# Three of four first layers by quarter products from the second group on, their weights' differences taken earlier, and some output adds done by DMA

## The chip, the core and the metric

The kernel runs on one core of a Trainium2 chip. The core has five engines with a queue of instructions each, worked off in order: TensorE (PE: matmuls into PSUM, with PEld for its weight loads), VectorE (DVE), ScalarE (ACT), GpSimd (POOL) and SyncE (SP), which here only issues DMAs. Engines meet through semaphores. The metric is the device time of one execution in microseconds (us); lower is better.

## The reference

Two stages. First, attention for 8 batches and 8 heads: 512 local tokens with a window of 32 to each side, plus 32 global tokens that see all and are seen by all. Second, a mixture of 8 experts on its output, with routing weights P from a Sinkhorn iteration:

```python
k_all = np.concatenate([k_g, k_l], axis=2); v_all = np.concatenate([v_g, v_l], axis=2)
out_g = np.matmul(sm(scale * q_g @ k_all.T), v_all)
s_ll = np.where(np.abs(pos[:, None] - pos[None, :]) <= 32, scale * q_l @ k_l.T, -1e9)
a_l = sm(np.concatenate([scale * q_l @ k_g.T, s_ll], axis=-1))
x = concat(out_g, a_l @ v_all)            # 4352 tokens, 512 wide
P = np.exp(x @ w_gate - max)
for _ in range(8):
    P /= P.sum(1, keepdims=True) + 1e-09
    P /= P.sum(0, keepdims=True) + 1e-09
    P *= N / E
for e in range(8):                        # w1[e]: 512 x 1024, w2[e]: 1024 x 512
    out += P[:, e:e + 1] * (np.maximum(x @ w1[e], 0.0) @ w2[e])
```

## The kernel before

**First part, about 0 to 374 us.** Attention runs in slots `s` of some 10.3 us, one pair of heads of one batch each (`HP` = 4 slots a batch, `NU` = 32). The matmuls of a slot are filled up with first layers of experts 0 to 3, one eighth at a time (`f1`, `p_l1`, L461 to L475); such a hidden tile `hT` (8 KB a partition, pool `hpool`, four buffers) is stored to DRAM (`hd`) when it is full. ScalarE and VectorE take the outputs in turn. SP issues the loads of queries and keys (`load_qk`, L122), of values (L166 to L172) and the hidden stores (L475), all in one queue. GpSimd issues the loads that change the type, among them `load_w1d` (L484): the first-layer weights of experts 4 to 7 are copied to DRAM in fp16 (`w1d`), one expert a batch from slot 13 on, in the order 4, 5, 6, 7. The Sinkhorn iterations follow, with the rest of the first layers beside them.

**Second part, about 374 us to the end.** Tokens come in groups `m` of 512 (0 to 7) and a last one of 256. Within a group the units (group, expert) come in `ORDER = (4, 0, 5, 1, 6, 2, 7, 3)`, that is in pairs (4,0), (5,1), (6,2), (7,3). The first unit of a pair computes its hidden layer now, the second loads it from `hd`. I call the body of the loop for the first unit the first half of the pair, for the second unit the second half. Everything is scaled by the routing weight `pb` on the way: the input `xs` (`scale_x`) or the loaded `h` (`scale_h`). The order of each engine's work is the order in which the loop body at the end writes it out.

The second layer is a 2x2 Strassen form: seven products (`product`, matmuls at L928) of h or sums and differences of halves of h (`sums`, VectorE at L689) with prepared weights `w2c`. Products 1 to 5 of a whole group accumulate in five fixed PSUM banks `m1` to `m5`; products 6 and 7 share rotating banks (`pm`) over the two units of a pair, so they are run back to back at a pair's middle: last in the first half, first in the second. `add` (L933) brings a finished bank into the output tile `o`: products 6 and 7 after each pair, products 1 to 5 once, after the pair (7,3) (`closes`). An add is one VectorE instruction (L944), and a first write is ScalarE's (L942). So ten VectorE adds stand together at the second half of (7,3): two for products 6 and 7, eight for the fixed banks. GpSimd then stores `o` (L947).

The first layer has two forms. The plain one, `l1` (L812), takes 32 matmuls of 512 columns a unit. The other, class `Fast` (L822), does it by quarter products: seven products of 256 columns for each half p of the hidden width, 56 matmuls of 256 columns in all. It needs weights as seven prepared quarters (`w1c`, in DRAM) and differences of quarters of `xs` (`sums_x`, four VectorE operations). A half p is done in four steps, s0 to s3, between the second-layer products:

```python
def s1(self):
    self.mul(self.K, 2, False, True)
    self.relu(self.K, 0, 0)
    self.mul(self.H, 6, False, True)
    self.X = self.tile("r1")
    nc.vector.tensor_tensor(out=self.X, in0=self.H, in1=self.t5, op=ALU.add)

def s2(self):
    self.mul(self.H, 7, False, True)
    self.mul(self.X, 3, False, True)
```

The VectorE add (L861) reads bank H, and the next matmuls of s2 add onto the same bank, so they wait for it. L868 is the second such add. A unit is `fast` from the group on that `WX` gives: experts 6 and 7 from group 2, twelve units in all. Half p = 0 of the next first unit is run in the first half of the pair ahead of it, half p = 1 in the second half. The prepared quarters are made in group 1: `load_w1` brings raw quarters, `prep_w1` (L735) takes four sums a piece on VectorE, and GpSimd stores them to `w1c`.

Of the kernel before, what the change touches and what calls it, by code (L numbers as in the profile page):

```python
# [9 lines left out]
FP16 = mybir.dt.float16  # L10
FP32 = mybir.dt.float32
AF = mybir.ActivationFunctionType
ALU = mybir.AluOpType
# [10 lines left out]
def kernel(  # L24
# [26 lines left out]
    HP = H // 2  # L51
    DP = D // P
    FT = F // P
    NT = NTOK // P
# [5 lines left out]

    persist = ctx.enter_context(tc.tile_pool(name="persist", bufs=1))
    lg = persist.tile([P, NT, E], FP32)
    wg_sb = persist.tile([P, DP, E], FP16)
    ones_f = persist.tile([P, P], FP32)
    identity = persist.tile([P, P], FP16)
# [5 lines left out]
    NL = E // 2  # L73
# [1 line left out]
    xd = [ydram.tile([P, DP, n], FP16, name=f"xd{m}") for m, (_, n) in enumerate(groups)]  # L75
    w1d = [ydram.tile([P, DP, F], FP16, name=f"w1d{e}") for e in range(NL, E)]
    pd = ydram.tile([E, NTOK], FP32, name="pd")
    WX = {6: 2, 7: 2}
    w1c = {e: [ydram.tile([P, 7, 2, 256], FP16, name=f"w1c{e}_{p}") for p in range(2)] for e in WX}
    psx = ExitStack()  # L80
    xpool = psx.enter_context(tc.tile_pool(name="xpool", bufs=1, side="right"))
    xT = [xpool.tile([P, DP, n], FP16, name=f"xT{m}") for m, (_, n) in enumerate(groups)]

    skp = ctx.enter_context(tc.tile_pool(name="skp", bufs=2))
    pss = ExitStack()
    ps_mm = pss.enter_context(tc.tile_pool(name="ps_mm", bufs=2, space=PSUM))
    ps_sc = pss.enter_context(tc.tile_pool(name="ps_sc", bufs=2, space=PSUM))
# [4 lines left out]
    with tc.tile_pool(name="att_c", bufs=1) as att_c, \  # L92
# [308 lines left out]
        def st_G1(b, g):  # L401
            n0 = HP * b + 2 * g
            qg = qgbd[(2 * b + g) % 2]
            gc = slice(Sg * b, Sg * (b + 1))
            sg = ps_po.tile([P, 2 * 512], FP32, tag="po")
            for c0, c1, k0 in ((0, Sl - W, 2 * W), (Sl - W, Sl, W), (Sl, S, None)):
                for pr in range(2):
                    rhs = kgT[:, 2 * g + pr, gc] if k0 is None else kTe[(n0 + pr) % NK][:, k0 : k0 + c1 - c0]
                    nc.tensor.matmul(sg[:, c0:c1], qg[:, pr, :], rhs, start=(pr == 0), stop=(pr == 1))
            m2 = att_wk.tile([P, 4], FP32, tag="m2")  # L410
            nc.vector.reduce_max(out=m2[:, 0:1], in_=sg[:, 0:S], axis=AX.X)  # L411
            nc.vector.tensor_scalar(out=m2[:, 1:2], in0=m2[:, 0:1], scalar1=-scale, scalar2=None, op0=ALU.mult)
# [64 lines left out]
        def load_w1e(e):  # L477
# [2 lines left out]
            wts[e] = pool.tile([P, DP, F], FP16, name="w1e", **kw)  # L480
            nc.gpsimd.dma_start(out=wts[e], in_=moe_w1[e].rearrange("(dko dki) f -> dki dko f", dki=P))

        def load_w1d(e):
            nc.gpsimd.dma_start(out=w1d[e - NL], in_=moe_w1[e].rearrange("(dko dki) f -> dki dko f", dki=P))  # L484

        fill = [(k % NL, k // NL) for k in range(NL * (B + 1))]
        n1 = 0
# [100 lines left out]
        for s in range(HP, NU + 1):  # L588
# [99 lines left out]
    def tt(out, in0, in1, op):  # L688
        nc.vector.tensor_tensor(out=out, in0=in0, in1=in1, op=op)  # L689
# [21 lines left out]
    raw = {}  # L711
    wnext = 0

    def load_w1(used):
        nonlocal wnext
        while wnext < len(wseq) and (wnext < 2 or wseq[wnext - 2] in used):
            i, *p = wseq[wnext]
            if p[0] is None:
                w = w1s[i] = wpool.tile([P, DP, F], FP16, tag="w1e", name="w1s")
                nc.sync.dma_start(out=w, in_=w1d[units[i][1] - NL])  # L720
            else:
                w = wpool.tile([P, 7, 2, 256], FP16, tag="w1e", name="w1q")
                if p[0] == "raw":
                    for o, r, k in ((0, 0, 0), (1, 0, 1), (3, 1, 0), (2, 1, 1)):
                        f0 = 512 * r + 256 * p[1]
                        nc.sync.dma_start(out=w[:, o], in_=w1d[i - NL][:, 2 * k : 2 * k + 2, f0 : f0 + 256])
                    raw[wseq[wnext]] = w
                else:
                    nc.sync.dma_start(out=w, in_=w1c[units[i][1]][p[0]])
                    w1s[(i, p[0])] = w  # L730
# [12 lines left out]

    def load_pb(*us):
        us = [i for i in us if i < NUN]
# [187 lines left out]
    def add(i, q, pm):  # L933
        m, e = units[i]
        nt = groups[m][1] // P // 2
        if m not in os_:
            os_[m] = ypool.tile([P, NJ, D], FP32, tag="y", name="o")
        for j, (r, d, sg) in enumerate(QUARTER[q]):
            o = os_[m][:, nt * r : nt * (r + 1), HD * d : HD * (d + 1)]
            p = pm[:, 0 : HD * nt].rearrange("p (t d) -> p t d", d=HD)  # L940
            if (q >= 6 and e == ORDER[1]) or (q in (3, 4) and j == 0):
                nc.scalar.mul(o, p, 1.0 / float(E))  # L942
            else:
                nc.vector.scalar_tensor_tensor(out=o, in0=p, scalar=sg / float(E), in1=o, op0=ALU.mult, op1=ALU.add)  # L944
# [128 lines left out]
    for i, (m, e) in enumerate(units):  # L1073
        if i == NUN - 1:
            last_pair(i)
        elif i % 2 == 0:
# [44 lines left out]
            else:  # L1121
# [92 lines left out]
```

## Time and profile before

| | us |
|---|---|
| median of 3 runs | 1045.3 |
| range of the runs | 1044.04 to 1048.0 |
| the profiled execution | 1044.08 |
| its span on the engines | 1042.2 |
| PE busy | 1015.2 |
| DVE busy | 868.7 |
| ACT busy | 513.0 |
| POOL busy | 139.7 |

The busy time of an engine is what its instructions took; matmuls overlap, so PE's is modelled. The prediction shows rows of four kinds. The page's first part gives busy time and share of the span. A window row gives, for a stretch of the span, its length, the busy time of each engine with its number of instructions, the TensorE clock that was granted (1.00 is full), the busy share of the DMA engines and GB/s. A timeline row gives start, length, engine, line, operation, output and inputs with sizes, how many were merged, and in brackets how long the engine had stood idle and what ended that.

### The profile page before, as it was taken

How to read it: one execution, taken by the hardware profiler on the slowest of the kernel's cores; microseconds unless marked ns; L12 is line 12 of the kernel's file. 1: busy time of each engine (PE TensorE's matmuls, PEld its weight loads, DVE VectorE, ACT ScalarE, POOL GpSimd, SP SyncE). 2: the span in 40 equal slices, each digit the busy share in tenths (PEclk: the TensorE clock that was granted, in tenths of full speed). 3: DMA queues.
4: the chain of work that ended last, by engine and by line, in shares of the span. 5: the costliest groups of instructions: out<-in, count | busy, mean ns of one | idle time of the engine just before them, and what ended most of it. 6: DMA issues, size and time to landing. Idle time of an engine off the chain costs nothing.

```text
span 1042.2 us, 22693 instructions
## 1 busy us (share of the span) xinstructions
PE 1015.2 (97%) x9142; PEld 728.5 (70%) x9142; DVE 868.7 (83%) x1638; ACT 513.0 (49%) x1296; POOL 139.7 (13%) x227
## 2 busy tenths in 40 slices
PE   7899999999999999999999999999999999999998
PEld 4555555555555466777777877877877878878887
DVE  7687777777776786999889799889899898898895
ACT  7777878787876675223222333333333332332331
POOL 7442423414312102000000000000000000000000
PEclk9899999999999999999999999999999999999999
DMA  9887588988945999946756546454553555464470
GB/s 260 197 217 207 118 273 181 220 232 177 258 136 142 275 261 302 259 143 203 272 194 234 189 153 219 160 189 180 200 189 138 203 187 168 172 218 152 145 260 26
DMA packets 101960, 206.08 MB, mean 198 GB/s; under 512 B 33936, under 2 KB 68192, under 8 KB 90592
## 3 DMA queue, kind: packets, MB, share of 16 engines
q1 hardware_dynamic: 56064, 162.75, 45.1%
q0 software_dynamic: 43184, 32.26, 17.7%
q10 hardware_dynamic: 2608, 9.64, 2.4%
q8 instruction: 71, 1.16, 0.4%
q14 instruction: 33, 0.27, 0.1%
HBM read 168.64 MB, written 57.29 MB: 217 GB/s over the span
## 4 chain that ended last, share of the span: by engine, by line
PE 83%; ACT 8%; DVE 6%; issue 2%; DMA 1%; SPq 0%; POOL 0%; ACTq 0%; DVEq 0%
PE m L928 28%; PE ph L818 15%; PE ph L468 15%; PE pm L928 11%; PE pf L836 7%; ACT Pu L311 4%; DVE Pu L348 3%; PE ptw L359 1%; ACT hT L471 1%; ACT qbd L285 1%; PE pv L157 1%; PE pt L275 1%; DMA vraw<-in_v_l_dram 1%; PE po L380 1%; DVE m L411 1%
## 5 line engine op out<-in xcount | busy, mean ns | idle before, releaser
L468 PE MATMUL ph<-xT,w1e 128*128 128x512 f16 (+1 forms) x1152 | 255.9, 367 | 0.2
L928 PEld LDWEIGHTS <-h 128*128 128x128 f16 x2160 | 211.4, 98 | 36.6
L820 ACT ACTIVATE h<-ph 128x512 f16<-128x512 f32 (+1 forms) x192 | 107.5, 562 | 204.2 <-PE ph L818 202.2
L928 PE MATMUL m<-w2c,s 128*128 128x256 f16 x1620 | 199.9, 273 | 0.0
L928 PEld LDWEIGHTS <-s 128*128 128x128 f16 x1620 | 158.5, 98 | 30.5
L818 PE MATMUL ph<-xs,w1s 128*128 128x512 f16 (+1 forms) x768 | 174.6, 361 | 0.0
L468 PEld LDWEIGHTS <-w1e 128*128 128x128 f16 x1152 | 105.4, 98 | 96.1 <-issue 3.0
L689 DVE TENSOR_TENSOR h<-h,pb 128x2048 f16<-128x2048 f16 (+1 forms) x48 | 152.4, 3175 | 3.8 <-DMA h<-hd 3.7
L689 DVE TENSOR_TENSOR s<-h 128x1024 f16<-128x1024 f16 (+2 forms) x166 | 126.4, 803 | 24.3 <-PE m L928 16.9
L928 PE MATMUL m<-w2c,h 128*128 128x256 f16 x1080 | 137.2, 273 | 0.0
L471 ACT ACTIVATE hT<-ph 128x512 f16<-128x512 f32 (+1 forms) x192 | 104.4, 559 | 47.5 <-PE ph L468 45.2
L928 PE MATMUL pm<-w2c,h 128*128 128x256 f16 x1080 | 123.8, 273 | 0.0
L818 PEld LDWEIGHTS <-w1s 128*128 128x128 f16 x768 | 75.1, 98 | 52.6
L843 ACT ACTIVATE h<-pf 128x512 f16<-128x512 f32 x96 | 55.0, 596 | 84.1 <-PE pf L836 79.9
L311 ACT ACTIVATE Pu<-ms,mx 128x160 f16<-128x160 f32 x224 | 93.6, 420 | 5.2 <-DVE mx L308 2.7
L473 DVE TENSOR_SCALAR hT<-ph 128x512 f16<-128x512 f32 x96 | 66.1, 688 | 31.3 <-PE ph L468 30.5
L689 DVE TENSOR_TENSOR h<-h 128x1024 f16<-128x1024 f16 (+1 forms) x166 | 90.3, 586 | 0.0
L689 DVE TENSOR_TENSOR xs<-xg,pb 128x2048 f16<-128x2048 f16 (+1 forms) x36 | 78.1, 2169 | 12.8 <-DMA pb<-pd 12.8
L947 POOL DMA_DIRECT2D out_dram<-o x8 | 6.1, 758 | 533.3 <-DVE o L944 533.3
L308 DVE CUSTOM_DVE_ANT_0 ms<-sc,mask 128x160 f32<-128x160 f32 x224 | 59.9, 319 | 18.7 <-PE sc L303 18.2
L836 PEld LDWEIGHTS <-w1q 128*128 128x128 f16 x672 | 65.7, 98 | 7.7
L852 ACT COPY pf<-pf 128x512 f32<-128x512 f32 x24 | 13.7, 570 | 81.5 <-PE pf L836 81.5
(165 smaller groups left out, 1225.7 us busy)
## 6 DMA issues: line engine op xcount, KB each, us to landing
h<-hd SPq DMA_DIRECT2D x32, 1024.0 KB
hd<-hT SPq DMA_DIRECT2D x26, 1024.0 KB
w1s<-w1d SPq DMA_DIRECT2D x24, 1024.0 KB
w1q<-w1c SPq DMA_DIRECT2D x24, 896.0 KB
pb<-pd SPq DMA_DIRECT2D x64, 256.0 KB
w2c<-in_moe_w_dram POOLq DMA_DIRECT2D x16, 512.0 KB, 20.1
out_dram<-o POOLq DMA_DIRECT2D x8, 1024.0 KB, 4.6
f<-in_q_l_dram SPq DMA_DIRECT2D x15, 512.0 KB
```

The costliest lines, as they stand in the source:

```text
L308: nc.vector.tensor_tensor_reduce(out=ms[:, ii, :], in0=sc[:, SW * ii : SW * (ii + 1)], in1=mask[:, mi, :], scale=-scale, scalar=BIG, op0=A ...
L311: nc.scalar.activation(out=d["Pu"][:, i, :], in_=ms[:, ii, :], func=AF.Exp, scale=-1.0, bias=d["mx"][:, i : i + 1], accum_out=d["sm"][:, i ...
L348: nc.vector.tensor_tensor(out=d["Pu"][:, i0:i1, 0:KW], in0=d["Pu"][:, i0:i1, 0:KW], in1=d["rs"][:, i0:i1].unsqueeze(2).to_broadcast([P, i1 ...
L468: nc.tensor.matmul(ph[:, 0:n], wts[e][:, dk, P * fm : P * (fm + 1)], xT[m][:, dk, :], start=(dk == 0), stop=(dk == DP - 1))
L471: nc.scalar.activation(out=hT[:, fm, 0:n], in_=ph[:, 0:n], func=AF.Relu)
L473: nc.vector.tensor_scalar(out=hT[:, fm, 0:n], in0=ph[:, 0:n], scalar1=0.0, scalar2=None, op0=ALU.max)
L689: nc.vector.tensor_tensor(out=out, in0=in0, in1=in1, op=op)
L818: nc.tensor.matmul(ph[:, 0:n], w1s[i][:, dk, P * fm : P * (fm + 1)], xss[i][:, dk, 0:n], start=(dk == 0), stop=(dk == DP - 1))
L820: nc.scalar.activation(out=hs[i][:, fm, 0:n], in_=ph[:, 0:n], func=AF.Relu)
L836: nc.tensor.matmul(bank[:, 256 * c : 256 * (c + 1)], self.w[:, self.sta[q], k, P * c : P * (c + 1)], self.mov[q][:, k], start=(first and c ...
L843: nc.scalar.activation(out=self.h[:, k : k + 2, 256 * c : 256 * (c + 1)], in_=bank.rearrange("p (k t) -> p k t", k=2), func=AF.Relu)
L928: nc.tensor.matmul(pm[:, HD * t : HD * (t + 1)], lhs[0][:, k, lhs[1] + P * t : lhs[1] + P * (t + 1)], w[:, k, q - 1, :], start=(k == 0 and ...
```

## The change

- `WX` becomes `{6: 1, 7: 1, 5: 1}`: experts 5, 6 and 7 are by quarter products from group 1 to group 7, 21 units in place of 12. Expert 5's half p = 0 is therefore run in the first half of the pair (4,0).
- The prepared quarters are made in the first part, in slots 16 to 28. In an even slot `wq_load` loads four raw quarters of a piece into a buffer of `hpool`; two sums stand at the end of the next (odd) slot, two at the end of the even slot after it, and then `wq_store` writes the piece. Loads and stores are on SP. The weights of experts 4 to 7 are copied in the order 6, 7, 5, 4. `prep_w1` and the raw loads of group 1 are gone.
- Products 6 and 7 of experts 1 and 2 (four a group) are no longer added by VectorE: ScalarE multiplies the bank into a new tile `a` (two buffers), and GpSimd issues a DMA that adds it to `o`.
- The pools `persist` and `skp` lie on the other side of the memory and are given back with `xpool`.

```diff
-    WX = {6: 2, 7: 2}
+    WX = {6: 1, 7: 1, 5: 1}
...
-    skp = ctx.enter_context(tc.tile_pool(name="skp", bufs=2))
+    skp = psx.enter_context(tc.tile_pool(name="skp", bufs=2, side="right"))
...
+        W1D = list(WX) + [e for e in range(NL, E) if e not in WX]
...
+        wqs = [(e, p) for e in WX for p in range(2)]
+        def wq_load(j):
+            if 0 <= j < len(wqs):
+                e, p = wqs[j]
+                w = wqt[j] = hpool.tile([P, 7, 2, 256], FP16, tag="hT", name="wq")
+                for o, r, k in ((0, 0, 0), (1, 0, 1), (3, 1, 0), (2, 1, 1)):
+                    f0 = 512 * r + 256 * p
+                    nc.sync.dma_start(out=w[:, o], in_=w1d[e - NL][:, 2 * k : 2 * k + 2, f0 : f0 + 256])
+        def wq_sums(j, part):
+            if 0 <= j < len(wqs):
+                w = wqt[j]
+                for o, a, b, op in ((5, 0, 3, ALU.subtract), (3, 3, 2, ALU.add), (4, 3, 0, ALU.subtract),
+                                    (6, 1, 4, ALU.subtract))[2 * part : 2 * part + 2]:
+                    nc.vector.tensor_tensor(out=w[:, o], in0=w[:, a], in1=w[:, b], op=op)
+        def wq_store(j):
+            if 0 <= j < len(wqs):
+                e, p = wqs[j]
+                nc.sync.dma_start(out=w1c[e][p], in_=wqt[j])
...
             if g1:
                 st_G1(*gn)
+            j, odd = divmod(s - 4 * HP, 2)
+            if odd:
+                wq_sums(j, 0)
+            else:
+                wq_sums(j - 1, 1)
+                wq_store(j - 1)
+                wq_load(j)
...
-                        load_w1d(b + 1)
+                        load_w1d(W1D[b - NL + 1])
...
-    for j, (e, p) in enumerate((e, p) for e in WX for p in range(2)):
-        wseq.insert(wseq.index((E + 2 * j + 2, None)), (e, "raw", p))
...
-    def prep_w1():
-        for k in list(raw):
-            w = raw.pop(k)
-            for o, a, b, op in ((5, 0, 3, ALU.subtract), (3, 3, 2, ALU.add), (4, 3, 0, ALU.subtract),
-                                (6, 1, 4, ALU.subtract)):
-                tt(w[:, o], w[:, a], w[:, b], op)
-            nc.gpsimd.dma_start(out=w1c[k[0]][k[2]], in_=w)
-            used.add(k)
...
-            if (q >= 6 and e == ORDER[1]) or (q in (3, 4) and j == 0):
+            if q >= 6 and e in ORDER[3:6] and m < B:
+                a = acp.tile([P, 2, HD], FP32, tag="a", name="a")
+                nc.scalar.mul(a, p, sg / float(E))
+                nc.gpsimd.dma_start(out=o, in_=a, accum_op=ALU.add)
+            elif (q >= 6 and e == ORDER[1]) or (q in (3, 4) and j == 0):
                 nc.scalar.mul(o, p, 1.0 / float(E))
...
+    acp = ctx.enter_context(tc.tile_pool(name="acp", bufs=2, reuse_waits="tile"))
...
-            if m > 0:
-                prep_w1()
```

More of the change, by code (lines that the diff above doesn't have):

```diff
@@ L59 @@
     scale = 1.0 / float(Dh) ** 0.5
[L63 to L67, printed above, removed]
     wpool = ctx.enter_context(tc.tile_pool(name="wpool", bufs=2))
@@ L77 @@
     pd = ydram.tile([E, NTOK], FP32, name="pd")
-    WX = {6: 2, 7: 2}
+    WX = {6: 1, 7: 1, 5: 1}
     w1c = {e: [ydram.tile([P, 7, 2, 256], FP16, name=f"w1c{e}_{p}") for p in range(2)] for e in WX}
     psx = ExitStack()
+    persist = psx.enter_context(tc.tile_pool(name="persist", bufs=1, side="right"))
+    lg = persist.tile([P, NT, E], FP32)
+    wg_sb = persist.tile([P, DP, E], FP16)
+    ones_f = persist.tile([P, P], FP32)
+    identity = persist.tile([P, P], FP16)
     xpool = psx.enter_context(tc.tile_pool(name="xpool", bufs=1, side="right"))
     xT = [xpool.tile([P, DP, n], FP16, name=f"xT{m}") for m, (_, n) in enumerate(groups)]
-    skp = ctx.enter_context(tc.tile_pool(name="skp", bufs=2))
+    skp = psx.enter_context(tc.tile_pool(name="skp", bufs=2, side="right"))
     pss = ExitStack()
@@ L481, in load_w1e @@
             nc.gpsimd.dma_start(out=wts[e], in_=moe_w1[e].rearrange("(dko dki) f -> dki dko f", dki=P))
+        W1D = list(WX) + [e for e in range(NL, E) if e not in WX]
         def load_w1d(e):
             nc.gpsimd.dma_start(out=w1d[e - NL], in_=moe_w1[e].rearrange("(dko dki) f -> dki dko f", dki=P))
+        wqs = [(e, p) for e in WX for p in range(2)]
+        wqt = {}
+        def wq_load(j):
[15 more added lines that the diff above has]
+                nc.sync.dma_start(out=w1c[e][p], in_=wqt[j])
         fill = [(k % NL, k // NL) for k in range(NL * (B + 1))]
@@ L708 @@
     wseq = [(i, p) for i in range(0, NUN, 2) for p in ((0, 1) if fast(i) else (None,))]
-    for j, (e, p) in enumerate((e, p) for e in WX for p in range(2)):
-        wseq.insert(wseq.index((E + 2 * j + 2, None)), (e, "raw", p))
-    raw = {}
     wnext = 0
@@ L722, in load_w1 @@
                 w = wpool.tile([P, 7, 2, 256], FP16, tag="w1e", name="w1q")
[L723 to L730, printed above, removed]
+                nc.sync.dma_start(out=w, in_=w1c[units[i][1]][p[0]])
+                w1s[(i, p[0])] = w
             wnext += 1
```

## The prediction

> **What bounds the kernel now.** I read the page's shares first, then the windows of one group of the second part, then the order of VectorE and TensorE inside it. The page:
>
> ```profile
> PE 1015.2 (97%) x9142; PEld 728.5 (70%) x9142; DVE 868.7 (83%) x1638; ACT 513.0 (49%) x1296; POOL 139.7 (13%) x227
> ```
>
> TensorE leaves 27 us of 1042.2. An average over both parts says little, so here are windows cut at the starts of the two leftover products 6 and 7 of each pair (columns: us, then busy time and count of PE, PEld, DVE, ACT, POOL, granted clock, DMA share, GB/s):
>
> ```profile
> 414.13:490.66 76.53, 76.53 (x578) 56.37 (x577) 71.49 (x75) 21.50 (x36) 1.31 (x2) 1.00 0.65 202
> 490.66:567.20 76.54, 76.54 (x579) 56.37 (x577) 67.09 (x71) 21.50 (x36) 2.38 (x4) 1.00 0.64 233
> ...
> 600.82:623.01 22.19, 22.19 (x175) 16.82 (x173) 20.72 (x22) 8.13 (x14) 0.00 (x0) 1.00 0.49 166
> 623.01:642.14 19.13, 19.13 (x146) 14.08 (x145) 18.92 (x25) 5.97 (x10) 0.76 (x1) 1.00 0.49 186
> 642.14:657.43 15.29, 15.29 (x143) 13.71 (x141) 12.19 (x12) 4.55 (x8) 0.00 (x0) 1.00 0.52 164
> 657.43:675.77 18.34, 18.34 (x170) 16.45 (x169) 16.01 (x25) 6.74 (x12) 0.00 (x0) 1.00 0.58 216
> ```
>
> TensorE is full in every window at full clock: it alone sets the time of the second part. A group with four plain first layers takes 76.53, one with two by quarter products 22.19+19.13+15.29+18.34 = 74.95. But VectorE is nearly as full where groups meet (18.92 of 19.13), and the order of its work there decides. VectorE's timeline across the boundary of groups 2 and 3 (start, us, line, operation, count, idle before):
>
> ```profile
> 610.08 0.70 DVE L868 TENSOR_TENSOR pf<-pf,c 128x512 f32<-128x512 f32 x1 [0.56 <-issue]
> 610.69 0.75 DVE L689 TENSOR_TENSOR h<-h 128x512 f16<-128x512 f16 x2
> 611.36 2.28 DVE L689 TENSOR_TENSOR h<-h,pb 128x2048 f16<-128x2048 f16 x1
> ...
> 620.41 4.42 DVE L689 TENSOR_TENSOR h<-h,pb 128x4096 f16<-128x4096 f16 x1
> 624.76 1.82 DVE L689 TENSOR_TENSOR s<-h 128x2048 f16<-128x2048 f16 x2
> 626.50 1.28 DVE L689 TENSOR_TENSOR h<-h 128x1024 f16<-128x1024 f16 x2
> 627.70 1.28 DVE L944 SCALAR_TENSOR_TENSOR o<-pm,o 128x512 f32<-128x512 f32 x2
> 628.90 5.06 DVE L944 SCALAR_TENSOR_TENSOR o<-m,o 128x512 f32<-128x512 f32 x8
> 633.88 1.82 DVE L689 TENSOR_TENSOR s<-h 128x2048 f16<-128x2048 f16 x2
> ```
>
> From 610.08, where it waited for TensorE, VectorE runs without a gap past the group's ten closing adds (627.70 to 633.88). Today nothing that TensorE needs soon stands behind them: pair (4,0) has a plain next layer, whose outputs ScalarE takes. Last, TensorE where a pair is followed by a first quarter-product layer (here (5,1) before expert 6):
>
> ```profile
> 567.03 3.66 PE L928 MATMUL pm<-w2c,h 128*128 128x256 f16 x32
> ...
> 574.89 0.60 PE L836 MATMUL pf<-xs,w1q 128*128 128x256 f16 x4
> ...
> 577.08 0.60 PE L836 MATMUL pf<-t,w1q 128*128 128x256 f16 x4
> ...
> 579.26 1.04 PE L836 MATMUL pf<-xs,w1q 128*128 128x256 f16 x8
> ```
>
> The batch at 579.26 first adds product 7 onto bank H, which VectorE must have read before (the add at L861). So 12.23 us after the start of products 6 and 7, TensorE needs that add done.
>
> **The change part by part.** *Nine more quarter layers* (expert 5 in groups 1 to 7, experts 6 and 7 in group 1). TensorE: (76.53-74.95)/2 = 0.79 us each, 9 x 0.79 = 7.1 us, all on the path. This is the gain. ScalarE: two copies a half, four a layer of 0.57 to 0.59 us, beside 21.50 busy of 76.53: hidden by its idle three quarters. VectorE: four adds of 0.70 (L861, L868) and four differences of x, 1.60 from start to start (639.14 to 640.74), about 4.3 a layer. Weights: twice 896 KB for 1024 KB, DMA share near 0.5: hidden.
>
> *Four adds of a group (products 6 and 7 of experts 1 and 2) to ScalarE and DMA.* VectorE loses 4 x 0.62 = 2.5 us a group, ScalarE gains 4 x 0.60. Each GpSimd DMA waits for ScalarE; behind it on that queue stands only the group's store. Two buffers, so expert 2's first multiply waits for a DMA issued a pair (18 us) before; the closing adds wait for expert 2's DMAs about 24 us after issue. The trace has no accumulating DMA; GpSimd DMAs of 896 and 1024 KB landed in 3.8 and 4.6 us (20.1 for the strided weights). Bounds for waiting: nothing, or the rival below. I take nothing. The VectorE time saved here lies mostly ahead of 610.08, where VectorE already waits for TensorE (0.66 and 0.56 idle): it buys waiting, not progress.
>
> *What now stands behind the closing adds.* Pair (4,0) is now followed by expert 5's quarter layer. In the changed order of VectorE, after L868 of pair (6,2) come: everything of 610.69 to 620.41 (9.72); four new differences for expert 5 (1.60); the scaling at 620.41 (4.35); sums (2.94); ten closing adds (6.18); sums of the second unit (1.73); and only then the add at L861 (0.70). That is 27.22, so it ends at 637.9. TensorE starts products 6 and 7 at 622.85 in its own list and wants the add 12.23 later, at 635.08. It waits 2.8 us; VectorE's waits for DMA inside this stretch (0.43, 0.23, 0.38 and 0.20 us before the scaling of x at later boundaries) make it 2.9. TensorE is in order, so second-layer products behind are late too, and no idle exists to absorb it. Once past it VectorE has caught up: its next add, in the second half, has over 1 us to spare. Six boundaries (1-2 to 6-7): 17.4 us. At boundary 0-1 VectorE is less late, but product 7's result is taken only at 475.06 to 475.67, and then 2.94+4.98+1.73+0.70 = 10.35 leads to 486.0, against 471.37+12.23 = 483.6: 2.4 us. Together 19.8. Boundary 7-8 has no quarter layer. Bounds for one boundary: zero, if VectorE overlaps more than I count, and 3.9, if the whole DMA wait seen at one boundary (0.43+0.79, with 2.8) counts.
>
> *The weights' differences in the first part.* The 16 sums of group 1 (0.42 each) and their 16 loads and 4 stores go: cover, not path, since TensorE was full there. In their place SP gets 24 loads of 128 KB and 6 stores of 896 KB, ahead of the next queries' loads and hidden stores, in slots 16 to 28 of 10.3 us; VectorE gets two sums (0.85) in each of 12 slots. In even slots a 1.22 us gap (before 219.26) covers them. In odd ones the gap is 0.34, so 0.5 us is late, with 0.62 and 1.13 of idle further on: 0 to 6 x 0.5 = 3 us. One of four hidden buffers is lent, so a tile reuses one two tiles old: the store issued at 254.84 must land by about 260.5 (3.3 us into the next slot), and a 1 MB load issued at 689.03 was waited for until 696.65: up to 2 us, once. DMA share is 0.81 to 0.96 there and the transfers add 8.6 MB to 27 MB in 123 us. Bounds 0 and 13 (below); I take 1.5, near zero as most slots have room.
>
> Memory moved to the other side costs no instruction. **Sum** against the profiled execution's 1044.1: 1044.1 - 7.1 + 19.8 + 1.5 = 1058.3. The median shown is 1045.3, 1.2 higher; I forecast 1059.0.
>
> **The rivals.** *VectorE is not late (faster).* The place is that one add. It decides if the stretch from 610.69 takes 24.4 us instead of 27.2. For: VectorE's total only goes from 68.0 of 74.95 to about 70 of 74.2 a group. Against: the stretch has no gap now, and the new items are counted from rows. It gives 1044.1-7.1+1.5 = 1038.5. Half late, some 1 us a boundary, gives 1045.5.
>
> *The first part becomes DMA-bound.* 8.6 MB at the 276 GB/s of its fullest stretch are 31 us of transfers; with 0.9 of the time taken, 123 us leave 12. If two thirds of the excess of 19 delay the end: 1058.3-1.5+12.7 = 1069.5. For: share 0.96 between 175 and 196 us. Against: 293 GB/s were moved at a share of 0.85 at 374 to 406, so the share is no hard limit.
>
> *The accumulating DMAs land late.* VectorE is gapless from 610.69 to 648; if descriptors wait for it, the closing adds stop at 627.70, the DMA then lands 3.8 later, in the stretch already late: 7 x 3.8 = 26.6 more, 1085. Against: 3.8 us was measured with VectorE busy, and two gaps follow the issue, at 607 and 609.5. The Trainium skill's page "SBUF — State Buffer", section "Who interferes with whom", says that GpSimd cannot write descriptors while VectorE holds the port pair both share; by its own exception for two-input operations, and by the row of 3.8 us, I give it little.
>
> **How the numbers follow.** 0.5% (5.2 us) is about what a measurement of this kernel can tell from no change: 1040.1 to 1050.5. Forecast, 0.62: own range 1052 to 1066 (a boundary of 2 to 3.9 us, the first part 0 to 3). First part DMA-bound, 0.12: 1062 to 1071. Not late, 0.12: 1037 to 1040. Half late, 0.10: 1041 to 1050. DMAs late, 0.04. So faster 0.12, same 0.10, slower 0.78. The range 1045 to 1069 leaves out the faster case, the late DMAs and a few hundredths at its ends.
>
> **What would show it.** Right: TensorE idle 2 to 4 us once a group, at L850 (the old L836), ended by VectorE's L875 (old L861); groups 2 to 6 at about 77 us where they were 74.95; VectorE's L875 directly after sums and ten L962 adds. Pairs followed by quarter layers elsewhere at 18.34 without a wait. The attention slots at 10.3 to 10.5 us. Wrong: no wait of TensorE on VectorE and groups of 74.2; VectorE waiting for a DMA at L962; or a longer first part with ScalarE or VectorE waiting for a store at the hidden tiles.

## The result and the profile after

The changed kernel takes 1085.7 us (median of 4 runs, 1084.2 to 1087.6), against 1045.4 us (1044.0 to 1048.0) for the kernel before, timed beside it: a ratio of 1.0395, 95% interval 1.0378 to 1.0411. The forecast was 1059.0 with a range of 1045 to 1069. The direction was right; the loss is three times as large as forecast, and outside the range.

The page of the profiled execution (span 1084.8 us; 1042.2 before):

```profile
PE 1023.8 (94%) x9358; PEld 752.8 (69%) x9358; DVE 888.6 (82%) x1731; ACT 551.2 (51%) x1364; POOL 177.5 (16%) x255
```

TensorE leaves 61 us idle where it left 27. It is also busy 8.6 us longer, although the change takes 7.1 us of matmuls away: some of them must have run slower. Next the windows, cut as before at the starts of products 6 and 7 of each pair (columns: us, then busy time and count of PE, PEld, DVE, ACT, POOL, granted clock, DMA share, GB/s). The first and the last are boundaries of two groups, from pair (7,3) to pair (4,0); the three between are one group:

```profile
642.75:663.05 20.30, 17.23 (x141) 14.32 (x140) 20.20 (x24) 4.61 (x8) 0.79 (x1) 0.92 0.50 177
663.05:681.39 18.34, 18.34 (x170) 16.43 (x168) 13.66 (x22) 7.93 (x14) 0.00 (x0) 1.00 0.59 187
681.39:700.63 19.24, 18.74 (x170) 16.34 (x168) 16.63 (x23) 7.88 (x15) 2.43 (x2) 1.00 0.62 172
700.63:722.82 22.19, 22.19 (x174) 16.77 (x172) 19.05 (x25) 9.47 (x17) 2.42 (x2) 1.00 0.71 237
722.82:741.42 18.60, 15.53 (x141) 13.69 (x140) 18.50 (x22) 4.66 (x8) 0.79 (x1) 1.00 0.56 192
```

Read this against the windows before: 15.29, 18.34, 22.19 and 19.13. The change takes half a first layer into the stretch behind (4,0) (15.29 becomes 18.34), and a whole plain one out of the boundary, where TensorE should then need 15.29, which is what the same set of products took in the kernel before. But VectorE has 18.1 to 18.5 us of work in the boundary, nearly as before, and so the boundary takes 18.2 to 18.6 at full clock. At the boundary of groups 2 and 3 it takes 20.30, since the granted clock is 0.92 there. The seven boundaries take 19.42, 21.95, 20.30, 18.60, 20.77, 18.24 and 18.23. The first, the second and the fifth of them are slow too:

```profile
481.84:501.26 19.42, 17.10 (x141) 14.55 (x140) 19.32 (x23) 4.67 (x8) 0.79 (x1) 0.91 0.52 183
561.03:582.98 21.95, 18.80 (x141) 15.14 (x140) 21.85 (x24) 4.61 (x8) 0.79 (x1) 0.84 0.46 163
801.24:822.01 20.77, 17.59 (x142) 14.45 (x141) 20.67 (x24) 4.71 (x8) 0.79 (x1) 0.92 0.50 172
```

Also, the pair behind (5,1) takes 19.24, not 18.34.

The timeline of VectorE and TensorE at the boundary of groups 2 and 3 (start, us, engine, line, operation, count, idle before and what ended it):

```profile
646.25 1.91 PE L942 MATMUL m<-w2c,h 128*128 128x256 f16 x16
...
649.96 1.28 DVE L962 SCALAR_TENSOR_TENSOR o<-pm,o 128x512 f32<-128x512 f32 x2
...
651.16 5.06 DVE L962 SCALAR_TENSOR_TENSOR o<-m,o 128x512 f32<-128x512 f32 x8
...
656.14 1.81 DVE L721 TENSOR_TENSOR s<-h 128x2048 f16<-128x2048 f16 x2
657.87 0.69 DVE L875 TENSOR_TENSOR pf<-pf,c 128x512 f32<-128x512 f32 x1
...
658.62 1.87 PE L850 MATMUL pf<-xs,w1q 128*128 128x256 f16 x8 [3.07 <-DVE pf L875]
...
660.28 2.50 PE L942 MATMUL m<-w2c,s 128*128 128x256 f16 x16
```

TensorE waits 3.07 us for the add at L875, which stands behind the ten closing adds, as forecast. Then it runs slowly: 16 matmuls take 2.50 us, where 16 of the same size took 1.91 at 646.25. Over the whole run TensorE's waits are these, in total, times, longest:

```profile
PE pf L850 <- DVE pf L875: 20.2, 7, 3.1
PE pt L428 <- DVE Pg L421: 11.2, 12, 3.1
...
PE pf L850 <- DMA w1q<-w1c: 1.8, 3, 0.8
```

The second was 2.9 in the kernel before and has grown in the first part. VectorE, TensorE and the queue of SP in attention slots 19 and 20:

```profile
200.01 4.83 SPq L497 DMA_DIRECT2D wq<-w1d  x4
...
211.62 0.88 DVE L504 TENSOR_TENSOR wq<-wq 128x512 f16<-128x512 f16 x2 [2.69 <-DMA wq<-w1d]
213.21 0.36 DVE L421 TENSOR_SCALAR Pg<-Pg,m 128x544 f16<-128x544 f16 x1
...
213.62 0.45 PE L428 MATMUL pt<-identity,Pg 128*128 128x128 f16 x5 [3.09 <-DVE Pg L421]
```

VectorE waits for the loads of a weight piece issued from 200 us on; the attention's Pg stands behind on VectorE, and TensorE waits for Pg.

So the 42.6 us of span split like this. The second part, counted here from its first products 6 and 7, begins at 424.44 instead of 413.97: 10.5 us are lost in the first part. From there to the end of the last window it is 653.64 instead of 621.62, 32.0 more: the saving of 7.1; 20.2 of waiting at the boundaries; 10.2 of slower matmuls there (the boundaries add up to 137.51; less 7 x 15.29 and less the waiting of 20.3 in those windows); 7 x 0.9 = 6.3 behind (5,1); and some 2.3 in the pairs behind (6,2), where weights w1q land late in the last groups. -7.1 + 20.2 + 10.2 + 6.3 + 2.3 = 31.9.

### The profile page after: what moved, and what is told of

Same layout as the page of the kernel before. It is cut to its first block, busy times and chain, and to the rows that moved or that the text cites. A ratio compares the mean times of both kernels' runs of the same rounds, so it can differ in the third digit from the quotient of the medians.

```text
span 1084.8 us, 23518 instructions
## 1 busy us (share of the span) xinstructions
PE 1023.8 (94%) x9358; PEld 752.8 (69%) x9358; DVE 888.6 (82%) x1731; ACT 551.2 (51%) x1364; POOL 177.5 (16%) x255
## 4 chain that ended last, share of the span: by engine, by line
PE 56%; DVE 25%; DMA 8%; ACT 5%; issue 4%; SPq 1%; POOL 0%; DVEq 0%; ACTq 0%
PE m L942 17%; PE ph L468 13%; PE pf L850 9%; PE pm L942 8%; DVE h L721 7%; PE ph L832 4%; DVE s L721 4%; DVE o L962 3%; DVE Pu L348 3%; DMA w1q<-w1c 3%; ACT Pu L311 2%; DMA wq<-w1d 2%; DMA pb<-pd 2%; DVE xs L721 2%; DVE pf L882 1%
## 5 line engine op out<-in xcount | busy, mean ns | idle before, releaser
L942 PE MATMUL m<-w2c,s 128*128 128x256 f16 x1620 | 206.3, 277 | 0.5
L857 ACT ACTIVATE h<-pf 128x512 f16<-128x512 f32 x168 | 97.3, 597 | 179.0 <-PE pf L850 147.1
L850 PEld LDWEIGHTS <-w1q 128*128 128x128 f16 x1176 | 115.7, 99 | 44.6 <-issue 26.7
L850 PE MATMUL pf<-xs,w1q 128*128 128x256 f16 x672 | 95.6, 276 | 22.2 <-DVE pf L875 20.2
L834 ACT ACTIVATE h<-ph 128x512 f16<-128x512 f32 (+1 forms) x120 | 64.5, 540 | 100.9 <-PE ph L832 98.8
L832 PE MATMUL ph<-xs,w1s 128*128 128x512 f16 (+1 forms) x480 | 103.7, 351 | 0.0
L958 POOL DMA_DIRECT2D o<-a x32 | 38.4, 1350 | 354.9 <-ACT a L957 354.8
L721 DVE TENSOR_TENSOR h<-h 128x512 f16<-128x512 f16 (+1 forms) x184 | 92.1, 542 | 0.0
L875 DVE TENSOR_TENSOR pf<-pf,c 128x512 f32<-128x512 f32 x42 | 29.3, 697 | 61.6 <-PE pf L850 40.4
L850 PE MATMUL pf<-t,w1q 128*128 128x256 f16 x504 | 76.6, 275 | 3.0 <-DVE pf L882 3.0
```

The costliest lines, as they stand in the source:

```text
L832: nc.tensor.matmul(ph[:, 0:n], w1s[i][:, dk, P * fm : P * (fm + 1)], xss[i][:, dk, 0:n], start=(dk == 0), stop=(dk == DP - 1))
L834: nc.scalar.activation(out=hs[i][:, fm, 0:n], in_=ph[:, 0:n], func=AF.Relu)
L850: nc.tensor.matmul(bank[:, 256 * c : 256 * (c + 1)], self.w[:, self.sta[q], k, P * c : P * (c + 1)], self.mov[q][:, k], start=(first and c ...
L857: nc.scalar.activation(out=self.h[:, k : k + 2, 256 * c : 256 * (c + 1)], in_=bank.rearrange("p (k t) -> p k t", k=2), func=AF.Relu)
L942: nc.tensor.matmul(pm[:, HD * t : HD * (t + 1)], lhs[0][:, k, lhs[1] + P * t : lhs[1] + P * (t + 1)], w[:, k, q - 1, :], start=(k == 0 and ...
L958: nc.gpsimd.dma_start(out=o, in_=a, accum_op=ALU.add)
```

## The experiments

All but the clock test start from the changed kernel, so each time is to be held against 1085.7.

**Four closing adds behind the bank add.** Is it the order of VectorE's work, or its amount?

```
 (odd unit that closes a group)
-                if q >= 6 or closes(i):
+                if q in (2, 1) and closes(i) and fast(i + 3):
+                    held.append((i, q, fixed[q]))
+                elif q >= 6 or closes(i):
                     add(i, q, fixed[q])
 ...
 (next even unit)
                     f.s1()
 ...
+                        for a in held:
+                            add(*a)
 ...
```

> The changed kernel with one thing moved: at the end of groups 0 to 6 the four VectorE adds that close products 2 and 1 (and the store of the output behind them) are issued after bank H's add of the next pair (L875 in the changed kernel) instead of ahead of it. Theory (TensorE's 20.2 us of waits at bank H's product 7 stand behind the ten closing adds, and the lower granted clock in the stretch behind them is a consequence of the wait): four adds of 0.63 us are 2.5 us a boundary, so of the seven waits (2.32 to 3.08 us) about 0.5 us each stays, some 3 us in all: about 17 us of waiting go, and with them most of the about 10 us of clock: 1085.7 - 17 - 10 = about 1059 us, granted clock 0.99 in the stretches where it was 0.84 to 0.92. Rival A (the clock drops there for another reason, say the matmuls themselves): waits go, clock stays: about 1069. Rival B (the wait is only moved to the second add, L882, or to products 2 and 1, which reuse the closed banks): above 1080.

Measured: 1076.8 us, ratio 1.0295 (1.0278 to 1.0313). The clock was 1.00 in every window, but the boundaries still took 16.9 to 18.3 us. One of them, in the windows:

```profile
713.00:730.88 17.88, 16.10 (x141) 13.66 (x140) 17.78 (x22) 4.53 (x8) 0.79 (x1) 1.00 0.50 155
```

VectorE is busy from end to end. The one wait of 3 us has become several short ones, and those, in total, times, longest, are:

```profile
PE pf L850 <- DVE pf L882: 8.4, 14, 0.8
PE pf L850 <- DVE pf L875: 4.0, 6, 0.7
```

So rival B held for the waits, and the theory for the clock: short waits cost no clock. The order decided how the loss came, in one long wait or in short ones; what still binds the boundary is how much VectorE has to do there.

**The same four adds left out.** This takes the amount away.

```
-                if q >= 6 or closes(i):
+                if q >= 6 or closes(i) and not (q < 3 and fast(i + 3)):
                     add(i, q, fixed[q])
```

> The changed kernel with the four closing adds of products 2 and 1 left out at the end of groups 0 to 6 (so a part of the output is missing; everything else is done). Moving these adds behind bank H's add gave 1076.8, not 1059: the waits came back at the other bank add. Theory now (capacity: in the stretch from the middle of pair (7,3) to the middle of pair (4,0) VectorE has about 18.4 us of work and no gap, TensorE now only 15.3 us, so about 3.1 us a boundary is lost wherever the adds stand): 4 x 0.63 = 2.5 us less VectorE work a boundary leaves about 0.6 us of waiting each, 4 in all, and no clock loss: 1085.7 - 17 - 10 = about 1059. Rival (the wait comes from the chain of product 6, bank add and product 7 itself and not from how much VectorE has to do): as with the adds moved, about 1077.

Measured: 1064.2 us, ratio 1.0188 (1.0161 to 1.0215); the boundaries take 15.4 to 17.0, together 114.8 instead of 137.5. One of them:

```profile
709.08:725.82 16.74, 15.92 (x141) 13.66 (x140) 16.64 (x19) 4.72 (x8) 0.79 (x1) 1.00 0.67 215
```

It is the theory's direction and most of its size: 21.5 of 27 us. The rival (1077) is out. What the theory missed is that VectorE is still the fuller engine in these windows, so 0.1 to 1.7 us remains at a boundary; also, the pairs behind (6,2) took 2.2 us more than in the changed kernel, with more waiting for w1q.

**The h scaling back in the first unit of pair (5,1).**

```
+                if not fast(i) or fast(i + 4):
+                    scale_h(i + 3, 0, HF)
                 if not fast(i):
-                    scale_h(i + 3, 0, HF)
                     product(i, 2)
 ...
-                late = fast(i - 1)
+                late = fast(i - 1) and not fast(i + 3)
```

> The changed kernel with one thing moved: the first half of the h scaling that the pair of experts (5,1) does in its second unit, ahead of its two bank adds, is done in the first unit again, as it was before the change; both halves in time, same work. Theory (these pairs take 19.24 us instead of 18.34 because the 2.28 us scaling stands ahead of the adds that TensorE waits for; in the first unit VectorE idles 2.29 us before its bank add): 0.9 x 7 = 6.3 us less, about 1079.4. Rival (the pair is slower since both its layers are quarter layers, whatever stands on VectorE): no change, 1085.7; or the add in the first unit is late in its place: 1085 to 1090.

Measured: 1080.0 us, ratio 1.0333 (1.0317 to 1.0348). The pair behind (5,1) is at 18.34 in every group; here in group 6, and the boundary that ends it:

```profile
916.36:934.70 18.34, 18.34 (x171) 16.43 (x169) 16.86 (x24) 7.94 (x15) 2.39 (x2) 1.00 0.81 245
...
956.88:975.83 18.95, 15.88 (x142) 13.66 (x141) 18.84 (x23) 4.72 (x8) 0.79 (x1) 1.00 0.53 188
```

So the 6.3 us behind (5,1) come from one scaling ahead of two adds. The times agree within the spread, partly by luck: the late weights behind (6,2) went as well, and the boundaries lost 4.8 us more, mostly by the clock.

**The four adds of a group on VectorE again.**

```
-            if q >= 6 and e in ORDER[3:6] and m < B:
-                a = acp.tile([P, 2, HD], FP32, tag="a", name="a")
-                nc.scalar.mul(a, p, sg / float(E))
-                nc.gpsimd.dma_start(out=o, in_=a, accum_op=ALU.add)
-            elif (q >= 6 and e == ORDER[1]) or (q in (3, 4) and j == 0):
+            if (q >= 6 and e == ORDER[1]) or (q in (3, 4) and j == 0):
```

> The changed kernel with one part undone: the four adds of a group that the change moved to ScalarE and accumulating DMAs are on VectorE again, as before the change (32 adds of 0.63 us, 20 us of VectorE in all). Theory (the move buys waiting, not progress: VectorE idles 2.15 to 2.73 us ahead of the bank adds in these pairs): 1085.7 within 3 us. Rival (VectorE is the bound in the pairs, each add is paid in full): up to 1085.7 + 20 = 1106.

Measured: 1089.5 us, ratio 1.0416 (1.0399 to 1.0434), 3.8 above the changed kernel where 3 was the bound and 20 the rival. The pairs behind (5,1), in which expert 1's adds stand again, are unchanged at 19.23 in all groups. The seven boundaries grew by 3.0 us, mostly by the clock. The pairs behind (6,2), with expert 2's adds, grew by 3.2, most of it waits for w1q (4.3 us in total instead of 1.8). The adds are not shown to be the cause of that: with the adds by DMA the same pairs took 1.0 to 2.4 us more than in the changed kernel in four of the runs described here. So VectorE's 20 us there bought waiting.

**Without expert 5's quarter products.**

```
-    WX = {6: 1, 7: 1, 5: 1}
+    WX = {6: 1, 7: 1}
```

> The changed kernel without expert 5's quarter products: experts 6 and 7 alone by quarter products, from group 1 on, with the differences of these two in the first part (four pieces instead of six); expert 5 computes its first layer directly, as before the change. Theory: the waits at the boundaries, the lower clock behind them and the 0.9 us in pairs (5,1) all come with expert 5 and go; what stays is the first part, some 4/6 of its 10.5 us = 7.0, and the gain of two more quarter layers, 2 x 0.79 = 1.6 us: 1045.4 + 7.0 - 1.6 = about 1051. Rival (the cost of the second part comes from the four adds by DMA or from the weights' place, not from expert 5): near 1075. Rival (the first part's 10.5 us is a threshold that four pieces stay under): about 1044.

Measured: 1053.0 us, ratio 1.0078 (1.0063 to 1.0093). Groups 1 to 6 take 74.94 to 75.01 at a clock of 1.00 without a wait: all the second part's loss comes with expert 5. The second part begins at 423.07, 9.1 us later than before, but the runs differ already ahead of the first piece. The same operation just before its load, in the kernel before, in the changed kernel and in this run:

```profile
167.21 0.37 DVE L421 TENSOR_SCALAR Pg<-Pg,m 128x544 f16<-128x544 f16 x1
```

```profile
167.61 0.36 DVE L421 TENSOR_SCALAR Pg<-Pg,m 128x544 f16<-128x544 f16 x1
```

```profile
168.69 0.36 DVE L421 TENSOR_SCALAR Pg<-Pg,m 128x544 f16<-128x544 f16 x1
```

Counted from this row, six pieces cost 10.1 us and four cost 7.6, where 7.0 was expected. The theory held within 2 us of the whole time, and neither rival did.

**The first part: sums left out, sums one slot later.** These two tell VectorE's waiting and VectorE's work from the load on the DMA engines.

```
 (sums left out)
+                nc.gpsimd.memset(w[:, 4:7], 0.0)
 ...
-                    nc.vector.tensor_tensor(out=w[:, o], in0=w[:, a], in1=w[:, b], op=op)
+                    pass

 (sums one slot later)
             if odd:
-                wq_sums(j, 0)
+                wq_sums(j - 1, 1)
+                wq_store(j - 1)
             else:
-                wq_sums(j - 1, 1)
-                wq_store(j - 1)
+                wq_sums(j - 1, 0)
                 wq_load(j)
```

> The changed kernel with VectorE's four sums per weight piece left out in the first part; the loads and the stores of the pieces stay, all bytes move (the places of the sums are filled with zeros by GpSimd; so experts 5, 6 and 7 compute with wrong weights). Theory A (the first part is 10.3 us longer because VectorE, in order, waits for late loads and spends 11.3 us on the sums, and Pg, Pu and TensorE wait behind it): the second part begins at 414 to 417 instead of 424.4, time 1076 to 1078. Theory B (the DMA engines are full, 0.98 of their time between 176 and 320 us, and everything that is loaded comes later): it begins at 422 to 424, time about 1084.

> The changed kernel with the sums of each weight piece one slot later (the first two in the next even slot, the other two and the store in the odd slot behind it), so that each load has two slots, about 20 us, instead of one. Same work. Theory A1 (VectorE's in-order wait for the loads is what costs): the waits of 4.6 us and what stands behind them go, the second part begins at about 417 to 419, time about 1079. Theory A2 (the sums' own 11.3 us on VectorE are the cost): 423 to 424, about 1085. Theory B (full DMA engines): 423 to 424, about 1085.

Measured, one run each: 1076.6 us with the second part beginning at 412.62, and 1083.7 with 417.97. The attention slots with weight pieces as windows, in the kernel before, the changed one, and without the sums:

```profile
176.00:320.00 144.00, 140.43 (x1559) 79.22 (x1559) 110.24 (x390) 117.27 (x371) 44.13 (x77) 1.00 0.82 207
```

```profile
176.00:320.00 144.00, 132.28 (x1451) 74.22 (x1449) 112.66 (x386) 108.38 (x342) 45.09 (x75) 0.99 0.98 261
```

```profile
176.00:320.00 144.00, 140.80 (x1560) 79.36 (x1559) 109.66 (x389) 117.69 (x372) 51.92 (x85) 1.00 0.98 264
```

Without the sums TensorE gets as much done in them as before the change (1560 matmuls), with the DMA engines as full as in the changed kernel (0.98, 264 GB/s). The waits between 160 and 330 us (in total, times, longest) in the kernel before, in the changed kernel, and with the sums one slot later:

```profile
PE pt L428 <- DVE Pg L421: 0.7, 3, 0.2
```

```profile
PE pt L428 <- DVE Pg L421: 9.0, 6, 3.1
ACT Pu L311 <- DVE mx L308: 8.7, 6, 3.1
DVE wq L504 <- DMA wq<-w1d: 4.6, 5, 2.7
```

```profile
PE pt L428 <- DVE Pg L421: 4.5, 7, 1.6
ACT Pu L311 <- DVE mx L308: 4.0, 6, 1.5
```

Theory A holds and B falls. With the sums later, VectorE's wait for the loads is no longer among the waits, and those behind it are halved. Counted from the row of Pg above (166.24 and 167.30 in these two runs), the first part takes 0.4 us less than in the kernel before without the sums, and 3.9 more with the sums later, against 10.1 more in the changed kernel. So 6.2 go when the loads get a second slot (VectorE's in-order wait); the other 3.9 are the sums themselves, in slots where TensorE waits for VectorE soon after. The second expected time (1079) was missed by 5 us: the second part took 657.3 us instead of 653.6 in that run, 2.2 more in the pairs behind (6,2) and 1.4 more in the boundaries.

**Waits of known length in the kernel before.** Extra copies on ScalarE, ahead of the one that a quarter layer's product 2 needs.

```
+            m, e = units[self.i]
+            if self.p == 1:
+                for _ in range({6: m + 1, 7: 10 - m}[e]):
+                    nc.scalar.copy(out=self.t5, in_=self.H)
             nc.scalar.copy(out=self.K, in_=self.H)
```

> The kernel before, with waits of known length put in front of TensorE: in the second half of the quarter layers of experts 6 and 7, extra copies of 0.6 us on ScalarE ahead of the copy that product 2 of the layer needs: 3 to 8 of them in groups 2 to 7 for expert 6, 8 to 3 for expert 7, so two waits of each length of about 1.3, 1.9, 2.5, 3.1, 3.7 and 4.3 us; the results stay the same. Theory (a wait of TensorE alone lowers the granted clock behind it, by chance of where it falls, from some length between 1.9 and 3.1 us on): waits of 1.3 and 1.9 leave the clock at 1.00 and cost only themselves; of 2.5 and 3.1 some cost up to 3.5 us more; 3.7 and 4.3 cost more nearly always. The added waits sum to 33.6 us; with clock losses of 1 to 3.5 us at six to eight of twelve, 1045 + 34 + 15 = about 1094. The Trainium skill, page "TensorE: Matmul & The Clock Gate", section "What's actually happening", gives one idle window of about 3.4 us as the condition for the halved clock; by that only the four waits above 3.4 us could cost more than themselves. Rival (the lower clock at the boundaries of the changed kernel has another cause than the wait): 1.00 behind all twelve, about 1079.

Measured, one run: 1091.0 us. The waits came out at 1.14 to 4.23 us. The windows of expert 6 in groups 3 to 7, of 18.34 us without a wait, with waits of 1.76, 2.38, 3.00, 3.61 and 4.23 us; behind them those of expert 7 in groups 2 to 5, of 22.19, with 4.23, 3.61, 3.00 and 2.38 (the three shortest, left out here, are at a clock of 1.00):

```profile
666.27:686.53 20.26, 18.50 (x171) 16.44 (x169) 16.01 (x25) 9.01 (x16) 0.00 (x0) 1.00 0.56 195
748.57:771.12 22.55, 20.17 (x171) 17.30 (x169) 16.02 (x25) 9.60 (x17) 0.00 (x0) 0.92 0.48 175
830.88:854.10 23.22, 20.22 (x170) 17.29 (x168) 15.96 (x24) 10.12 (x18) 0.00 (x0) 0.93 0.50 170
913.25:938.22 24.97, 21.36 (x171) 17.77 (x169) 16.01 (x25) 10.77 (x19) 0.00 (x0) 0.86 0.45 158
996.74:1021.14 24.40, 20.17 (x171) 17.29 (x168) 16.01 (x25) 11.35 (x20) 0.00 (x0) 0.93 0.41 146
602.79:631.85 29.06, 24.83 (x175) 17.98 (x172) 20.74 (x22) 12.75 (x23) 0.00 (x0) 0.88 0.37 127
686.53:714.16 27.63, 24.02 (x175) 17.67 (x173) 19.46 (x22) 12.17 (x22) 0.00 (x0) 0.94 0.39 133
771.12:796.46 25.34, 22.34 (x174) 16.84 (x172) 19.99 (x22) 11.58 (x21) 0.00 (x0) 1.00 0.40 146
854.10:878.83 24.73, 22.35 (x175) 16.82 (x172) 20.35 (x23) 11.14 (x20) 0.00 (x0) 1.00 0.44 149
```

Take 18.34 or 22.19 from the busy time: waits up to 1.76 us never cost more than 0.2 beside themselves; of the four of 2.38 and 3.00, two cost 1.8 to 1.9 more; the four of 3.61 and 4.23 cost 1.8 to 3.0 more, all of them. The theory holds, and the rival is out: a wait alone lowers the clock. The Trainium skill, page "TensorE: Matmul & The Clock Gate", section "What's actually happening", gives one idle window of about 3.4 us as the condition for the halved clock. The trace differs, since waits of 2.38 and 3.00 were enough in two cases of four. An estimate from that page, half the clock for one such window, is a loss of 1.7 us. That is near four of the six losses here, of 1.8 to 1.9. Why one wait of 3.00 lowers the clock and another does not stays open.

**Boundary work on GpSimd.** Could the amount be moved? Half or all of the h scaling ahead of the closing sums (the second form is shown; `scale_h` now takes the engine).

```
-            scale_h(i + 3)
+            scale_h(i + 3, eng=nc.gpsimd if fast(i + 4) else None)
```

> The changed kernel with work taken off VectorE at the boundaries without leaving anything out: the second half of the h scaling (128x2048, 2.2 us on VectorE) that stands ahead of the closing sums at the end of a group is done by GpSimd, which has 5.6 us of work in a group of 78. Theory (capacity: VectorE has 18.4 us of work there for TensorE's 15.3): the seven waits of about 3 us shrink to about 0.9 us each and the clock stays at 1.00: 20.2 - 6.3 = 14 and 10 us less, about 1062. Rival (GpSimd is too slow, or slows VectorE while it runs, so that the sums behind the scaling wait for it instead): 1075 to 1090.

> The same with the whole of that h scaling (128x4096, 4.4 us on VectorE) on GpSimd. Theory: the waits at the boundaries are gone altogether, with the clock loss: 1085.7 - 20 - 10 = about 1056. Rival (GpSimd needs more than the about 13 us until the sums of that tile are due, or slows VectorE): the sums wait for GpSimd, 1070 to 1095.

Measured, one run each: 1101.7 and 1107.2 us, worse than the bounds of theory and rival. GpSimd takes 4.08 us for a half that took VectorE 2.28, and VectorE's next operation stands still while it runs. The boundary with half, then with all of the scaling moved:

```profile
641.01 4.08 POOL L824 TENSOR_TENSOR h<-h,pb 128x2048 f16<-128x2048 f16 x1 [14.71 <-PE ph L832]
641.17 4.20 DVE L721 TENSOR_TENSOR xs<-xs 128x512 f16<-128x512 f16 x1
```

```profile
728.68 8.07 POOL L824 TENSOR_TENSOR h<-h,pb 128x4096 f16<-128x4096 f16 x1 [16.77 <-DMA h<-hd]
729.38 9.04 DVE L721 TENSOR_TENSOR s<-h 128x2048 f16<-128x2048 f16 x2 [0.50 <-ACT h L834]
```

A difference of 0.42 us takes 4.20, and sums of 1.82 us take 9.04: the operation that meets GpSimd's ends only after it. So moving 2.2 us off VectorE costs it 3.8 there.

**A version without expert 5 whose pieces cost less.** First the sums one slot later, then all four pieces at the end of the first part.

```
 (first: as "sums one slot later" above, with)
-    WX = {6: 1, 7: 1, 5: 1}
+    WX = {6: 1, 7: 1}
 (second: besides)
-            j, odd = divmod(s - 4 * HP, 2)
+            j, odd = divmod(s - 7 * HP, 2)
 ...
         sk_cols(cp)
+        if it in (2, 5):
+            j = 2 + it // 5
+            wq_sums(j, 0)
+            wq_sums(j, 1)
+            wq_store(j)
+            wq_load(j + 1)
```

> The changed kernel without expert 5's quarter products (1053.0, second part beginning at 423.1) and with the sums of the weight pieces one slot later in the first part, as tried with six pieces, where the second part then began 6.5 us earlier. Theory (the first part loses by VectorE's in-order waits for late loads, mostly with the first pieces): the second part begins at about 417, the rest as without expert 5: 1053.0 - 6 = about 1047, still 0.3 % over the kernel before, since the sums' own time on VectorE stays. Rival (with four pieces the loads are in time and the sums alone cost): about 1053.

> The kernel without expert 5's quarter products again, with the four weight pieces of experts 6 and 7 taken to the end of the first part: two in the last slots of the attention (slots 28 to 33, where the DMA engines are busy a quarter of the time in the kernel before), two between the steps of the loop over the gate's normalisation, where TensorE is busy throughout and VectorE 75 % of the time. Theory (the pieces cost only where VectorE's work in the attention slots is what TensorE waits for): the second part begins 0 to 2 us later than before the change and is 1.6 us shorter: 1043 to 1045, the same as the kernel before within what a measurement can tell. Rival (the loads come late there, since the DMA engines are full from 340 us on, and VectorE's normalisation waits behind them): 1048 to 1055.

Measured: the first 1046.1 us, ratio 1.0016 (1.0007 to 1.0025), and every group runs without a wait. The second part begins at 420.00, not 417, but 3.8 us of that stand ahead of the first piece (the row of Pg is at 170.99 here): the four pieces cost 2.2 us instead of 7.6. The time confirms the theory within 1 us. The second 1061.2 us, ratio 1.0156 (1.0135 to 1.0178), worse than the rival's range. Its two pieces in the last slots cost about 1 us; with the two in the gate's loop TensorE is busy only 27.5 of the 40 us from 350 to 390, where it was busy 39.5 before. Two waits there (ScalarE's and VectorE's, in total, times, longest):

```profile
ACT hT L471 <- DMA xg<-xd: 11.0, 1, 11.0
...
DVE wq L504 <- DMA wq<-w1d: 8.0, 3, 4.1
```

VectorE waits for the pieces, as the rival said. ScalarE, which the rival had not thought of, is shown to wait 11 us until a load named xg<-xd; why that came to stand ahead of it was not followed further. No version beat the kernel before: the best is 0.2% slower.

## Why the prediction was right and wrong

- *Nine more quarter layers, -7.1 us.* Right. Without expert 5 the two layers of group 1 gave 76.5 to 75.0; and behind (4,0) and at the boundary TensorE's own work is what was forecast.
- *What now stands behind the closing adds, +19.8 us.* Right in place and size: 20.2 us, seven waits of 2.3 to 3.1, each ended by L875 behind ten adds. But the reason given, the order, is only part of it. Moving four adds behind the bank add left 18 us of the loss; leaving them out removed most. It is simpler to see in the windows: VectorE 18.9 of 19.13 before, and a change that lowers TensorE's side to 15.3.
- *"TensorE is in order ... and no idle exists to absorb it"*: the price of a wait was taken to be its length. This failed. Waits of 2.3 to 3.1 us also lowered the clock behind them in four of seven boundaries, 10.2 us that the sum had no term for. With this and the next point, groups 2 to 6, forecast at about 77 us, took 78.4 to 80.6.
- *"Pairs followed by quarter layers elsewhere at 18.34 without a wait."* Wrong: 19.24 behind (5,1), 6.3 us in all. With expert 5 a quarter layer, a condition in the unchanged code (`late = fast(i - 1)`) becomes true for this pair and puts a scaling of 2.28 us ahead of its two bank adds. Undone, 18.34. The prediction costed VectorE's new operations but did not ask which old conditions read the changed table.
- *The weights' differences in the first part, +1.5 us, bounds 0 and 13.* The term that was mis-sized most: 10.5. The step that failed is "0.5 us is late": it priced the sums' time in a slot and took their loads as landed. VectorE waited up to 2.7 us for them with Pg behind it. That is 6.2; the sums' own time, priced at 0 to 3, is 3.9; 0.4 of the 10.5 stand ahead of the first piece.
- *"Weights: ... hidden."* Wrong by some 2.3 us: behind (6,2) TensorE waited for w1q in the last groups, 1.8 us in total.
- *"The slots at 10.3 to 10.5 us."* Wrong for the same reason: up to 12.9.
- *The four adds by DMA: "buys waiting, not progress".* Right, as far as shown. The windows behind (5,1) stayed at 19.2 with expert 1's adds on either engine.
- *Rival: the first part becomes DMA-bound (1069).* Its size was near (12.7 against 10.5) by luck; its mechanism is wrong: with all transfers and no sums the first part lost nothing.
- *Rival: the accumulating DMAs land late (1085).* Its time is the one measured, by accident. They landed in 5.4 us in the median and no add waited for them.
- *Rival: VectorE is not late, or half late.* Refuted: the boundaries are late in full.

The range was too narrow because each term's bounds were of its own mechanism: four terms (the clock, the condition, the late loads of the pieces, the late weights) were missing, all of the same sign.

## What to carry to other kernels

Before taking TensorE work out of a stretch, hold the busy time of every other engine in that same stretch against what is left: here the boundary took no less than VectorE's work in it, 18.2 us in the changed kernel and 16.9 to 18.3 with four adds moved behind, where TensorE alone needed 15.3. A new operation on an in-order engine costs not only its own time but the wait for its data as well, paid by everything queued behind it; give a load more than the time it takes in the fullest stretch. And search the unchanged code for each condition that reads what the change alters.

## What the runs showed of the hardware

- TensorE's clock can fall after a wait of as little as 2.3 us. In the test 2.38 and 3.00 us did it in two of four cases, 3.61 and 4.23 in four of four, 1.76 and less in none; each fall cost 1.8 to 3.5 us more, in the test and in the changed kernel. In the changed kernel the clock of a boundary was 0.91 with a wait of 2.32, and with waits of 3.07 it was 0.84, 0.92 and 1.00. The moved adds, with waits of 0.8 us at most, left it at 1.00.
- A VectorE operation on two SBUF operands stood still while GpSimd ran one on two SBUF operands: 0.42 us became 4.20 beside one of 4.08, 1.82 became 9.04 beside one of 8.07. The Trainium skill, page "SBUF — State Buffer", section "Who interferes with whom", says that a VectorE instruction with two SBUF inputs contends with a GpSimd instruction that reads SBUF, and that the second to issue blocks; the trace agrees.
- A DMA that accumulates 256 KB from SBUF into SBUF landed in 5.4 us in the median, with an issue of 1.2 us on GpSimd, while VectorE was busy 86% of the second part, and no add of VectorE waited for one.
